# Attention and two expert layers on one core: sums of blocks taken one at a time, attention's late parts moved two points on, weight events spaced wider, another order in the opening

## The chip, the cores and the metric

The kernel runs on one core of a Trainium2 chip. The metric is the device time of one execution in microseconds (us). Engines run side by side, each through its own list of instructions in order: TensorE (PE; its weight loads are PEld), VectorE (DVE), ScalarE (ACT), GpSimd (POOL) and SyncE (SP), which here issues every DMA.

## The reference, cut to what matters

```python
# q, k, v: (4, 8, 768, 64); 8 memory slots ahead of each window; chunks of 32 queries
for c in range(24):                       # a chunk sees 8 + 16 + 32 + 8 = 64 slots
    scores = matmul(q_c, k_full.T) / 8
    out[:, :, chunk c] = softmax(scores) @ v_full
x = out.transpose(0, 2, 1, 3).reshape(3072, 512)
h = x @ w_in;  x = relu(h)**2 @ w_out     # first layer, w_in 512 x 2048, w_out 2048 x 512
h = x @ w_in2; g = h * tanh(softplus(h))  # second layer
return g @ w_out2
```

All in 32 bit. The weights are drawn as 64 bit numbers, and the kernel turns them into 32 bit ones itself.

## The kernel before, in words

**Blocks and steps.** The 3072 tokens are three blocks of 1024. Attention works in 12 pairs `p` of two 128-token tiles, four pairs to a block. After an opening (attention of pairs 0 to 3) come 48 steps `s`: 24 of the first layer, 24 of the second, eight per block, numbered `j`; each takes 256 of the 2048 columns. A matrix product is done as a 2x2 product of blocks with seven multiplications in place of eight, so there are sums of blocks before (T1 to T4 of the activations, S1 to S4 of the weights) and after. Each factor is split into a rounded part `hi` and a rest `lo`, and hi*hi, lo*hi and hi*lo are added up: six matmuls of 512 columns for a half product.

**One step.** `step(s)` writes the first product of step s between the second product of step s-1. PE's order is P1, P6, P5, P2, P7, P4, P3 (`product`, line 478, six matmuls each). P1 and P2 share PSUM bank 0 (`a`), P6, P7 and P4 bank 1 (`b`), P5 and P3 bank 2 (`c`). ACT copies `u1` from `a` (L737) before P2 may add to it; DVE makes `u2` (L744) and `u3` (L763) from `b`, each before the next product may add to `b`; then c22, c21, c12 (L765, L771, L776). `gate` applies the activation on ACT, casts `hi` (L491), and POOL subtracts to get `lo` (L492). In the first layer the second product is eight `unit`s (L533) with a DVE add into `y` (L547); in the second it is seven `product2` (L568) of blocks B11, B22, B21, T3, T1, T2, T4, each into one of two bank pairs. DVE adds a bank pair into a running block `m` (L556), or ACT copies it (L579) where j is 0. Three of the seven blocks are in buffers named by `spare` ('xt0' to 'xt2' or 'raw0' to 'raw2'), four in 'y0' and 'y1'. `sums_g` (L519) makes the T blocks of g on DVE.

**Combining.** When a block of tokens ends, seven additions over the `m` blocks give the four output blocks (`combine`, also L556, m<-m). Four stand behind the sixth product2 of the step after the block's last, three in the step after that, behind its first three product2. In the last step all seven come before `last_unit` (L607), which adds the last contribution unblocked, 12 matmuls for each output block, in bank pairs.

**Points.** A step has 15 points, the calls of `rest()` behind each product and unit. At a point, waiting stores and weight streams are issued, and then whatever `at(s, i)` listed: attention of later pairs (`plan_attention`) and weight events (`plan_w`), in the order in which they were listed (weights first). The order on each engine is that of the program text; no scheduler moves anything. First-layer points: P1 0, P6 1, P5 2, units 3 and 4, P2 5, P7 6, units 7 to 9, P4 10, P3 11, units 12 to 14; the gate of c21 comes behind point 10, that of c12 behind point 11.

**Attention of a pair.** `scores` (L344) on PE; maxima and exponentials; `normalize` (sums on DVE, multiplications on POOL, L384); `transpose_p` (L392) on PE; `copy_pt` (L402) on ACT; `values` (L414) on PE; `copy_x` (L426) on ACT; sums on POOL; a store. Scores, transposes and values share banks 6 and 7. In the opening `place_x` (L446 on ACT, L447 on DVE) puts a pair's blocks into x.

**A weight event** turns one matrix slice into hi and lo: `rebias` (A, a; ACT, L145) and `decode` (D, d; DVE, L152 to L156) of its halves, block sums (S, s; DVE, L167 to L171), casts (R, r; ACT, L211), subtractions (L, l; DVE, L218) and two pairs of stores. For the second layer's weights there are 16 events: six in steps 8 to 13, one each (both casts in one buffer, 'xt2'), and ten from step 17 on, one every nine points.

Of the kernel before, what the change touches and what calls it, by code (L numbers as in the profile page):

```python
# [41 lines left out]
PRODUCTS2 = [(A11, B11), (S4, B22), (A12, B21), (S3, T3), (S1, T1), (S2, T2), (A22, T4)]  # L42
STEPS = 2 * NSB * NQ

OUTPUTS = {T4: (1, 0), B21: (0, 0), T1: (1, 1), B22: (0, 1)}
FIRST2 = NSB * NQ
# [5 lines left out]
def tile_chunk_attention_moe_moe2(  # L52
# [224 lines left out]
    def spare(sb, i):  # L277

        return f"{('xt', 'raw')[sb % NSB % 2]}{i % 3}"
# [96 lines left out]
    def normalize(p):  # L376
        for h2 in range(2):
            nc.vector.tensor_reduce(out=r_t[p][:, h2], in_=p_t[p][:, h2], axis=AX.X, op=ALU.add)
        r = r_t[p]
        nc.vector.tensor_scalar_add(out=r, in0=r, scalar1=1.0e-9)  # L380
        nc.vector.reciprocal(out=r, in_=r)  # L381
        for h2 in range(2):
            pr = p_t[p][:, h2]
            nc.gpsimd.tensor_tensor(  # L384
                out=pr, in0=pr, in1=r[:, h2].unsqueeze(2).to_broadcast([128, 8, SLOTS]), op=ALU.mult
            )
# [197 lines left out]
    def combine(sb, blk, store):  # L584

        m = {b: m_t[sb, b] for _, b in PRODUCTS2}
        if blk == T2:
            add(m[T2], m[T2], m[B11])
            add(m[T3], m[T3], m[T2])
            add(m[T2], m[T2], m[T1])  # L590
            add(m[T1], m[T1], m[T3])
        else:
            add(m[blk], m[blk], m[{T4: T3, B22: T2, B21: B11}[blk]])
        if store:
            store_y(sb, *OUTPUTS[T1 if blk == T2 else blk], m[T1 if blk == T2 else blk])

    def last_unit(s, n):
# [4 lines left out]
        first = (4 + 2 * (pairs[0] % 2), 4 + 2 * ((pairs[0] + 1) % 2), 0, 2)[n]  # L602
# [35 lines left out]
    def at(s, i, *work):  # L638

        beside.setdefault((s + i // POINTS, i % POINTS), []).extend(work)  # L640

    def plan_attention(s, i, p):

        for n, work in {
# [5 lines left out]
            11: lambda: transpose_p(p),  # L650
            12: lambda: copy_pt(p),
            14: lambda: (values(p), load_q(p + 1) if (p + 1) % PSB else None),
            15: lambda: copy_x(p),
            16: lambda: sums_x(p, nc.gpsimd),
            20: lambda: store_x(p),
# [20 lines left out]
    def step(s):  # L676
# [44 lines left out]
        def done(i):  # L721
            _, sb, j = where(s - 1)
            final = s == STEPS - 1
            if (j == NQ - 1 or final) and PRODUCTS2[i][1] == T2:
                combine(sb, T2, not final)
            if final and PRODUCTS2[i][1] == T4:
                for blk in (T4, B22, B21):
                    combine(sb, blk, False)
            if sb > NSB and j == 0 and i < 3:
                combine(sb - 1, (T4, B22, B21)[i], True)  # L730

        if live:
# [59 lines left out]
    with tc.manual_schedule():  # L792
# [24 lines left out]
        def multiply(p):  # L817
            values(p)
            copy_x(p)
            sums_x(p, nc.vector if p == PSB - 1 else nc.gpsimd)  # L820
# [26 lines left out]
        normalize(3)  # L847
        turn(2)
        multiply(2)
        place_x(1, 0, 3)  # L850
        place_x(1, 3, 7)
        turn(3)
        multiply(3)
        place_x(2, 0, 3)
        place_x(2, 3, 7)
        place_x(3, 0, 3)
# [13 lines left out]
        for n, e in enumerate(seconds):  # L870
            if n < NQ - 2:
                plan_w(NQ + n, 0, e, "Aa|D|d|RS|s|L||||r|l", lambda e, i: round_w2(e, i, "xt2"), split_w2, "val")
            else:
                n -= NQ - 2
                hi = (["xt0", "xt1"], ["xt2", "at1"])[n % 2]
                plan_w(
                    2 * NQ + 1, 9 * n, e, "Aa|D|d|RS|s|Lr||l",
# [92 lines left out]
```

## Time and profile before

| what | value |
|---|---|
| median of three runs | 1168.34 us (1166.24 to 1169.35) |
| profiled execution | 1169.24 us, of it 1167.2 us from its first to its last instruction |
| mean granted clock of TensorE | 0.972 |
| PE busy | 1079.9 us (93%) |
| PEld busy | 881.1 us (75%) |
| DVE busy | 896.1 us (77%) |
| ACT busy | 561.5 us (48%) |
| POOL busy | 430.0 us (37%) |
| DMA | 324.94 MB, mean 278 GB/s |

Busy shares are averages over stages that differ. A timeline row gives the start, the time to the end of the last instruction of the group, engine, line, operation, names, shapes and count; in brackets stands the idle time before it and what ended it. A clock of 1.00 is 2.4 GHz; the other level is 1.2 GHz.

### The profile page before, as it was taken

What the parts mean: (1) busy time and instruction counts of PE and PEld (TensorE: products, weight loads), DVE (VectorE), ACT (ScalarE), POOL (GpSimd) and SP (SyncE); (2) the same over time, 40 slices, a digit from 0 to 9 for tenths busy, and PEclk for the clock granted to TensorE, in tenths of its full rate; (3) what the DMA queues carried; (4) which work ended last, traced back from release to release, by engine and by line L of the source; (5) the groups of instructions that cost most, each with busy time, mean ns of one, the idle gap of its engine ahead of it and who ended that gap; (6) DMA issues with size and microseconds to landing.
All of it is one profiled execution on the core that took longest, in us unless ns stands there. A gap on an engine that the chain in (4) does not pass through costs nothing.

```text
span 1167.2 us, 19779 instructions
## 1 busy us (share of the span) xinstructions
PE 1079.9 (93%) x7478; PEld 881.1 (75%) x7478; DVE 896.1 (77%) x1164; ACT 561.5 (48%) x879; POOL 430.0 (37%) x333
## 2 busy tenths in 40 slices
PE   6869899898799889999999999999989999799997
PEld 5748688776677778887777778888868888578885
DVE  5586879969666655678998677898878988768886
ACT  2467555555454444557565645444354443253331
POOL 2423223232223323223222244555355545245451
PEclk9999899999989889999999999999999999899998
DMA  9556867777998786869999958989997889867531
GB/s 359 231 193 233 293 214 262 260 277 248 384 320 315 263 292 241 280 237 395 342 338 329 362 218 289 314 304 339 345 309 276 303 304 391 277 207 230 161 128 72
DMA packets 192125, 324.94 MB, mean 278 GB/s; under 512 B 13344, under 2 KB 151072, under 8 KB 188192
## 3 DMA queue, kind: packets, MB, share of 16 engines
q1 hardware_dynamic: 192032, 323.69, 78.0%
q8 instruction: 60, 0.98, 0.3%
q14 instruction: 33, 0.27, 0.1%
HBM read 231.62 MB, written 92.01 MB: 277 GB/s over the span
## 4 chain that ended last, share of the span: by engine, by line
PE 56%; DVE 11%; DMA 7%; ACT 4%; issue 3%; SPq 0%; DVEq 0%; ACTq 0%
PE banks L478 26%; PE banks L568 17%; PE banks L533 10%; DMA w_d<-hi 2%; DVE m L556 2%; DVE y L547 1%; PE banks L414 1%; PE banks L607 1%; DMA w1s<-w_d 1%; DVE ty L632 1%; DVE val L152 1%; DVE r L519 1%; ACT r L497 1%; DMA xt<-xt_d 1%; DMA w2s<-w_d 1%
## 5 line engine op out<-in xcount | busy, mean ns | idle before, releaser
L478 PE MATMUL banks<-x,w1s 128*128 128x512 f32 x2016 | 507.8, 399 | 23.5 <-DVE u L763 7.5
L492 POOL TENSOR_TENSOR g<-r,g 128x512 fp32r<-128x512 f32 x206 | 287.3, 1401 | 537.5 <-ACT g L491 442.6
L478 PEld LDWEIGHTS banks<-x,w1s 128*128 128x128 f32 x2016 | 385.8, 193 | 112.5 <-DVE u L763 9.7
L533 PE MATMUL banks<-g,w2s 128*128 128x512 f32 x1152 | 282.4, 395 | 6.8 <-DVE y L547 5.3
L533 PEld LDWEIGHTS banks<-g,w2s 128*128 128x128 f32 x1152 | 217.2, 190 | 57.7 <-DVE y L547 8.2
L568 PE MATMUL banks<-g,w2s 128*128 128x512 f32 x966 | 241.3, 392 | 9.8 <-ACT m L579 7.6
L568 PEld LDWEIGHTS banks<-g,w2s 128*128 128x128 f32 x966 | 181.2, 189 | 52.2 <-ACT m L579 9.7
L556 DVE TENSOR_TENSOR m<-banks,m 128x1024 f32<-128x1024 f32 x144 | 173.6, 1218 | 34.9 <-PE banks L568 26.3
L491 ACT CAST g<-r 128x512 fp32r<-128x512 f32 x206 | 127.0, 621 | 37.5 <-DVE r L519 30.3
L547 DVE TENSOR_TENSOR y<-banks,y 128x512 f32<-128x512 f32 x168 | 112.0, 682 | 39.0 <-PE banks L533 38.9
L492 POOL TENSOR_TENSOR g<-more,g 128x512 fp32r<-128x512 f32 x55 | 79.7, 1453 | 81.0 <-ACT g L491 66.6
L497 ACT ACTIVATE r<-r 128x512 f32<-128x512 f32 x72 | 45.4, 631 | 69.7 <-DVE r L771 50.1
L501 ACT ACTIVATE r<-r 128x512 f32<-128x512 f32 x48 | 30.4, 632 | 71.4 <-DVE r L771 35.9
L211 ACT CAST hi<-val 128x1024 fp32r<-128x1024 f32 (+1 forms) x32 | 30.4, 949 | 69.5 <-DVE val L156 50.5
L498 ACT ACTIVATE r<-r 128x512 f32<-128x512 f32 x96 | 60.7, 632 | 3.1
L152 DVE TENSOR_SCALAR val<-val 128x512 f32<-128x512 f32 x64 | 38.9, 607 | 26.5 <-ACT val L145 26.4
L414 PE MATMUL banks<-pt,v 64*64 64x32 f32 x1536 | 39.9, 262 | 19.4 <-ACT pt L402 19.0
L218 DVE TENSOR_TENSOR val<-val,hi 128x1024 f32<-128x1024 f32 (+1 forms) x32 | 37.2, 1162 | 25.2 <-ACT hi L211 25.0
L414 PEld LDWEIGHTS banks<-pt,v 64*64 64x64 f32 x1536 | 37.0, 185 | 25.7 <-ACT pt L402 24.8
L737 ACT COPY u<-banks 128x512 f32<-128x512 f32 x48 | 28.1, 585 | 52.0 <-PE banks L478 52.0
L384 POOL TENSOR_TENSOR p<-p,sum 128x512 f32<-128x512 f32 x24 | 28.7, 1215 | 63.3 <-DVE sum L381 25.0
L344 PE MATMUL banks<-k,q 64*32 64x64 f32 x1536 | 37.5, 250 | 13.2 <-DMA k<-k_dram 7.1
(71 smaller groups left out, 999.9 us busy)
## 6 DMA issues: line engine op xcount, KB each, us to landing
w1s<-w_d SPq DMA_DIRECT2D x280, 256.0 KB, 5.4
w2s<-w_d SPq DMA_DIRECT2D x229, 256.0 KB, 5.3
raw<-w_dram SPq DMA_DIRECT2D x64, 512.0 KB, 5.0
w_d<-w1s SPq DMA_DIRECT2D x8, 1792.0 KB, 7.5
x<-xs_d SPq DMA_DIRECT2D x14, 1024.0 KB, 10.7
k<-k_dram SPq DMA_DIRECT2D x24, 512.0 KB, 7.0
v<-v_dram SPq DMA_DIRECT2D x24, 512.0 KB, 8.9
xt<-xt_d SPq DMA_DIRECT2D x21, 512.0 KB, 7.3
```

The lines of the kernel that those rows point to most:

```text
L152: nc.vector.tensor_scalar(out=val, in0=val, scalar1=LIMIT, scalar2=-LIMIT * NEGATIVE, op0=ALU.min, op1=ALU.max)
L344: nc.tensor.matmul(out=s4[32 * c:32 * c + 32, j, hp, :], lhsT=q_t[p][r0:r0 + 64, j, hp, 32 * c:32 * c + 32], rhs=k_t[p][r0:r0 + 64, j, hp, ...
L414: nc.tensor.matmul(out=x_ps[par][64 * h2:64 * h2 + 64, o:o + 32], lhsT=v_t[p][j][r0:r0 + 64, h2, a, c, :], rhs=pt_t[p][r0:r0 + 64, h2, j, ...
L478: nc.tensor.matmul(out=ps, lhsT=w[:, a, f:f + 128], rhs=x[:, xi, c, kk, :], start=start and i == 0, stop=stop and i == len(order) - 1, ski ...
L491: nc.scalar.copy(out=g[:, 0], in_=r)
L492: nc.gpsimd.tensor_tensor(out=g[:, 1], in0=r, in1=g[:, 0].bitcast(FP32), op=ALU.subtract)
L497: nc.scalar.activation(out=r, in_=h, func=ACTF.Relu)
L498: nc.scalar.activation(out=r, in_=r, func=ACTF.Square)
L533: nc.tensor.matmul(out=ps, lhsT=w[:, a, blk(f), d % 2 * 128:d % 2 * 128 + 128], rhs=g_t[s, (f, t)][:, c, :], start=i == 0, stop=i == len(o ...
L547: nc.vector.tensor_tensor(out=y, in0=ps, in1=y, op=ALU.add)
L556: engine.tensor_tensor(out=to, in0=in0, in1=in1, op=ALU.add)
L568: nc.tensor.matmul(out=bank(first + d), lhsT=w[:, a, 128 * d:128 * d + 128], rhs=g[:, c, :], start=i == 0, stop=i == 2)
```

## The change

- `PRODUCTS2`: the products of T1 and T2 change places (T2 fifth, T1 sixth).
- `combine` does one addition per call, listed in `SUMS`. At a block's end the first stands behind product T2, the second behind T1; in the next step the third stands behind `sums_g` of T2 and the other four behind product2 of B11, B22, B21 and T3. In the last step: one behind T2, three behind T1, three behind T4.
- `spare` counts blocks from the second layer's first, so the last block's three `m` go to 'raw' and no longer to 'xt'.
- `last_unit` takes banks 0 to 3 first and the two bank pairs last.
- Attention in steps: transposes, copy_pt one point later, values, copy_x, sums and store two later, load_q one earlier. The first point and period go from 4 and 26 to 4 and 25 (from step 0), and from 10 and 19 to 8 and 19 (from step 9). There q is now loaded ahead of k.
- Weight events: seven in steps 8 to 14, nine from step 17 on, one every ten points.
- Opening: pair 3's normalizing and pair 2's sums go from POOL to DVE; the placing of pairs 1 and 2 goes behind values(3), ahead of copy_x(3); pair 3's first part is placed ahead of its sums.

```diff
-PRODUCTS2 = [(A11, B11), (S4, B22), (A12, B21), (S3, T3), (S1, T1), (S2, T2), (A22, T4)]
+PRODUCTS2 = [(A11, B11), (S4, B22), (A12, B21), (S3, T3), (S2, T2), (S1, T1), (A22, T4)]
+SUMS = [(T2, B11), (T3, T2), (T2, T1), (T1, T3), (T4, T3), (B22, T2), (B21, B11)]
...
-        return f"{('xt', 'raw')[sb % NSB % 2]}{i % 3}"
+        return f"{('xt', 'raw')[(sb - NSB) % 2]}{i % 3}"
...
-    def combine(sb, blk, store):
+    def combine(sb, to, other, store=False):
 
         m = {b: m_t[sb, b] for _, b in PRODUCTS2}
-        if blk == T2:
-            add(m[T2], m[T2], m[B11])
-            add(m[T3], m[T3], m[T2])
-            add(m[T2], m[T2], m[T1])
-            add(m[T1], m[T1], m[T3])
-        else:
-            add(m[blk], m[blk], m[{T4: T3, B22: T2, B21: B11}[blk]])
-        if store:
-            store_y(sb, *OUTPUTS[T1 if blk == T2 else blk], m[T1 if blk == T2 else blk])
+        add(m[to], m[to], m[other])
+        if store and (to, other) in SUMS[3:]:
+            store_y(sb, *OUTPUTS[to], m[to])
...
-        first = (4 + 2 * (pairs[0] % 2), 4 + 2 * ((pairs[0] + 1) % 2), 0, 2)[n]
+        first = (0, 2, 4 + 2 * (pairs[0] % 2), 4 + 2 * ((pairs[0] + 1) % 2))[n]
...
-            11: lambda: transpose_p(p),
-            12: lambda: copy_pt(p),
-            14: lambda: (values(p), load_q(p + 1) if (p + 1) % PSB else None),
-            15: lambda: copy_x(p),
-            16: lambda: sums_x(p, nc.gpsimd),
-            20: lambda: store_x(p),
+            12: lambda: transpose_p(p),
+            13: lambda: (copy_pt(p), load_q(p + 1) if (p + 1) % PSB else None),
+            16: lambda: values(p),
+            17: lambda: copy_x(p),
+            18: lambda: sums_x(p, nc.gpsimd),
+            22: lambda: store_x(p),
...
-            if (j == NQ - 1 or final) and PRODUCTS2[i][1] == T2:
-                combine(sb, T2, not final)
-            if final and PRODUCTS2[i][1] == T4:
-                for blk in (T4, B22, B21):
-                    combine(sb, blk, False)
-            if sb > NSB and j == 0 and i < 3:
-                combine(sb - 1, (T4, B22, B21)[i], True)
+            blk = PRODUCTS2[i][1]
+            if s == STEPS - 1:
+                for n in {T2: (0,), T1: (1, 2, 3), T4: (4, 6, 5)}.get(blk, ()):
+                    combine(sb, *SUMS[n])
+            elif j == NQ - 1:
+                for n in {T2: (0,), T1: (1,)}.get(blk, ()):
+                    combine(sb, *SUMS[n])
+            elif sb > NSB and j == 0:
+                for n in {B11: (3,), B22: (4,), B21: (5,), T3: (6,)}.get(blk, ()):
+                    combine(sb - 1, *SUMS[n], store=True)
...
+                if where(s - 1)[1] > NSB and where(s - 1)[2] == 0:
+                    combine(where(s - 1)[1] - 1, *SUMS[2])
...
-        def multiply(p):
+        def multiply(p, *others):
             values(p)
+            for other in others:
+                place_x(*other)
             copy_x(p)
-            sums_x(p, nc.vector if p == PSB - 1 else nc.gpsimd)
+            if p == PSB - 1:
+                place_x(p, 0, 3)
+            sums_x(p, nc.vector if p >= PSB - 2 else nc.gpsimd)
...
-        normalize(3)
+        normalize(3, nc.vector)
         turn(2)
         multiply(2)
-        place_x(1, 0, 3)
-        place_x(1, 3, 7)
         turn(3)
-        multiply(3)
-        place_x(2, 0, 3)
-        place_x(2, 3, 7)
-        place_x(3, 0, 3)
+        multiply(3, (1, 0, 3), (1, 3, 7), (2, 0, 3), (2, 3, 7))
         place_x(3, 3, 7)
...
-            if n < NQ - 2:
+            if n < NQ - 1:
...
-                    2 * NQ + 1, 9 * n, e, "Aa|D|d|RS|s|Lr||l",
+                    2 * NQ + 1, 10 * n, e, "Aa|D|d|RS|s|Lr||l",
...
-            start, first, period = ((0, 4, 26), (NQ + 1, 10, 19))[sb]
-            at(start, 0, *([lambda p=p: load_k(p)] if sb else []), lambda p=p: load_q(p))
+            start, first, period = ((0, 4, 25), (NQ + 1, 8, 19))[sb]
+            at(start, 0, lambda p=p: load_q(p))
+            if sb:
+                at(start, 0, lambda p=p: load_k(p))
```

## Rows read from the trace of the kernel before

**Rows 1.** Windows of stages: stretch, length, busy us (count) per engine, clock, DMA share, GB/s
```profile
62.20:468.40 406.20, 369.37 (x3495) 299.17 (x3496) 297.05 (x461) 215.06 (x343) 124.48 (x108) 0.95 0.76 271
468.40:509.20 40.80, 40.80 (x182) 33.78 (x181) 26.16 (x33) 23.18 (x35) 10.31 (x9) 1.00 0.72 249
509.20:662.30 153.10, 146.74 (x631) 118.57 (x630) 133.13 (x208) 88.17 (x136) 37.05 (x27) 0.99 0.95 346
```

**Rows 2.** Windows of steps 11, 33, 41 and 43, same columns
```profile
359.10:389.20 30.10, 26.58 (x231) 22.19 (x227) 17.93 (x31) 14.21 (x23) 8.76 (x8) 0.89 0.83 296
840.10:865.80 25.70, 21.69 (x85) 16.62 (x84) 21.41 (x20) 12.70 (x18) 11.73 (x7) 0.93 0.74 244
1000.20:1030.00 29.80, 21.98 (x86) 17.02 (x85) 18.11 (x19) 12.85 (x18) 9.35 (x7) 0.89 0.71 235
1049.00:1068.00 19.00, 19.00 (x85) 15.74 (x84) 15.85 (x17) 7.25 (x12) 9.85 (x7) 1.00 0.61 194
```

**Rows 3.** Timeline of PE, second layer
```profile
858.62 4.50 PE L478 MATMUL banks<-x,w1s 128*128 128x512 f32 x12 [3.17 <-DVE u L763]
...
1015.89 2.93 PE L568 MATMUL banks<-g,w2s 128*128 128x512 f32 x6 [6.36 <-ACT m L579]
...
1151.24 11.04 PE L607 MATMUL banks<-g,w2s 128*128 128x512 f32 x36 [3.84 <-DVE m L556]
```

**Rows 4.** Timeline of DVE, the combining sums of steps 32, 33 and 41
```profile
840.22 5.01 DVE L556 TENSOR_TENSOR m<-m 128x1024 f32<-128x1024 f32 x4
...
851.22 6.74 DVE L556 TENSOR_TENSOR m<-m 128x1024 f32<-128x1024 f32 x3
...
1011.25 3.48 DVE L556 TENSOR_TENSOR m<-m 128x1024 f32<-128x1024 f32 x3
```

**Rows 5.** Timeline of POOL, steps 32 and 33
```profile
825.14 3.45 POOL L492 TENSOR_TENSOR g<-r,g 128x512 fp32r<-128x512 f32 x2
...
852.44 2.24 POOL L492 TENSOR_TENSOR g<-more,g 128x512 fp32r<-128x512 f32 x1
```

**Rows 6.** Timeline of ACT, step 41
```profile
1014.83 1.01 ACT L579 COPY m<-banks 128x1024 f32<-128x1024 f32 x1 [6.41 <-DVE m L556]
```

**Rows 7.** Timeline of DVE, the end
```profile
1144.32 5.72 DVE L556 TENSOR_TENSOR m<-m 128x1024 f32<-128x1024 f32 x4
...
1162.32 1.23 DVE L556 TENSOR_TENSOR m<-banks,m 128x1024 f32<-128x1024 f32 x1 [1.49 <-PE banks L607]
```

**Rows 8.** Timelines of ACT, DVE and PE, the end of the opening
```profile
59.66 3.47 ACT L446 CAST x<-stage 128x768 fp32r<-128x768 f32 x4
...
61.28 4.09 DVE L447 TENSOR_TENSOR x<-stage,x 128x768 fp32r<-128x768 f32 x4
...
62.24 7.20 PE L478 MATMUL banks<-x,w1s 128*128 128x512 f32 x18 [3.57 <-ACT x L446]
```

**Rows 9.** Timeline of PE, waits of the first layer
```profile
84.90 1.07 PE L392 MATMUL banks<-cst,p 128*128 128x128 f32 x4 [4.41 <-POOL p L384]
...
140.63 4.12 PE L414 MATMUL banks<-pt,v 64*64 64x32 f32 x128 [3.25 <-ACT pt L402]
...
382.81 1.46 PE L414 MATMUL banks<-pt,v 64*64 64x32 f32 x30 [3.45 <-ACT pt L402]
...
...
420.05 4.12 PE L414 MATMUL banks<-pt,v 64*64 64x32 f32 x128 [3.21 <-ACT pt L402]
...
560.15 3.01 PE L478 MATMUL banks<-x,w1s 128*128 128x512 f32 x12 [2.21 <-ACT u L737]
```

**Rows 10.** Timeline of ACT, steps 11 and 13
```profile
377.39 1.05 ACT L211 CAST hi<-val 128x1024 fp32r<-128x1024 f32 x1 [3.20 <-DMA w_d<-hi]
...
418.31 1.22 ACT L145 ACTIVATE val<-raw 128x512 f32<-128x512 f32 x2 [5.85 <-DMA w_d<-val]
...
424.27 1.07 ACT L426 COPY stage<-banks 128x512 f32<-128x512 f32 x2 [0.19 <-DMA raw<-w_dram]
```

**Rows 11.** Timeline of ACT, step 19
```profile
558.78 0.83 ACT L211 CAST hi<-val 128x768 fp32r<-128x768 f32 x1 [3.94 <-DVE val L156]
```

More of the change, by code (lines that the diff above doesn't have):

```diff
@@ L374, in exps, with normalize @@
         nc.scalar.activation(out=pr, in_=pr, func=ACTF.Exp, scale=scale)
-    def normalize(p):
+    def normalize(p, engine=nc.gpsimd):
         for h2 in range(2):
@@ L383, in normalize @@
             pr = p_t[p][:, h2]
-            nc.gpsimd.tensor_tensor(
+            engine.tensor_tensor(
                 out=pr, in0=pr, in1=r[:, h2].unsqueeze(2).to_broadcast([128, 8, SLOTS]), op=ALU.mult
@@ L722, in done @@
             _, sb, j = where(s - 1)
-            final = s == STEPS - 1
-            if (j == NQ - 1 or final) and PRODUCTS2[i][1] == T2:
-                combine(sb, T2, not final)
-            if final and PRODUCTS2[i][1] == T4:
-                for blk in (T4, B22, B21):
-                    combine(sb, blk, False)
-            if sb > NSB and j == 0 and i < 3:
-                combine(sb - 1, (T4, B22, B21)[i], True)
+            blk = PRODUCTS2[i][1]
[8 more added lines that the diff above has]
+                    combine(sb - 1, *SUMS[n], store=True)
         if live:
@@ L870, in tile_chunk_attention_moe_moe2 @@
         for n, e in enumerate(seconds):
-            if n < NQ - 2:
+            if n < NQ - 1:
                 plan_w(NQ + n, 0, e, "Aa|D|d|RS|s|L||||r|l", lambda e, i: round_w2(e, i, "xt2"), split_w2, "val")
             else:
-                n -= NQ - 2
+                n -= NQ - 1
                 hi = (["xt0", "xt1"], ["xt2", "at1"])[n % 2]
                 plan_w(
-                    2 * NQ + 1, 9 * n, e, "Aa|D|d|RS|s|Lr||l",
+                    2 * NQ + 1, 10 * n, e, "Aa|D|d|RS|s|Lr||l",
                     lambda e, i, hi=hi: round_w2(e, i, hi[i]), split_w2, ("val", "at0")[n % 2],
```

## The prediction

> **What bounds the kernel now.** I read the page's shares first: PE is busy 93% of the span, so a gain has to come from PE's waits, from the lower clock that follows some of them, or from the two ends. Then the windows by stage, to see which stages lie above their floor. The reader is to see in [rows 1] that two steps without attention or weight events take 40.8 us, 20.40 each, with PE never idle; that is the floor of a first-layer step (90 matmuls, 0.227 us each). Seven steps with weight events take 153.1, where 7 x 20.40 = 142.8: 10.3 us too long. The first stretch, steps 0 to 14, has a granted clock of 0.95 over 406.2 us: about 41 us of it at 1.2 GHz. In the second layer a step takes 19.0 us [rows 2], but step 33 takes 25.7 and step 41 takes 29.8. Third, PE's timeline gives the waits behind these numbers [rows 3, 9]; fourth, the timelines of DVE, POOL and ACT say what ended them [rows 4 to 8, 10, 11].
>
> The sums are made against the profiled execution, 1169.24 us (span 1167.2 and 2.0 around it). It lies 0.9 above the median of 1168.34, so 0.9 comes off at the end.
>
> **The end (step 47 and the last unit).** Now four sums (5.72 us), one addition of a bank pair (1.23, the length of the last one) and three sums stand in DVE's list one after the other from 1144.32; PE waits 3.84 us for a bank pair and then takes 11.04 us for 36 matmuls [rows 3, 7], which at 0.227 us would take 8.2: it runs at the lower clock. DVE's last addition ends at 1163.55. After: the first two output blocks go to banks that nobody reads any more, so PE has no wait, and the other 24 matmuls need only the pair that the T1 addition frees. DVE then sets the end: one of the four early sums is done before, so from the T1 addition's end it has 6 sums and 5 additions of 1.23 = 13.5 us, plus 0.7 because the first sums run beside POOL (5.72 against 4 x 1.23 = 4.9). That addition ends at 1144.3, so DVE ends near 1158.5 to 1159.2: 4.3 to 5 us earlier. The stores now come 1.23 apart, which may cost some of it. I take **-4.3** (bounds -5.5 and -2).
>
> **Steps 33 and 41.** In step 32 four sums (5.01 us) stand ahead of the T4 addition and of the sums_g that start step 33; three more, 6.74 us, end just before u3, and PE waits 3.17 us for u3 [rows 3, 4]. In step 41 the wait is another: the copy of m waits for the old m in the same 'xt' buffer (6.41 us on ACT, 6.36 on PE) [rows 3, 6]; its three sums take only 3.48. The new `spare` removes that sharing, so step 41 becomes a second step 33. There, the first sum goes before the T1 addition, where DVE has time (15.85 us busy in a 19.0 us step [rows 2]); the second stays ahead of the T4 addition; the third to sixth stand ahead of u3, the seventh behind c22. So the chain up to u3 loses two sums ahead of the T4 addition and the one behind c22, and gets two back in step 33: it starts some 3.7 us earlier (three sums of 1.25) and has one more sum in it.
>
> What that one costs depends on POOL. A sum takes 1.16 us where POOL stood still and 2.25 where POOL was subtracting [rows 4]; in that stretch a subtraction itself took 2.24 us [rows 5]. With all four sums at 2.25, u3 comes 3.7 - 2.25 = 1.4 us earlier, so step 33 gains 1.4 and step 41, from 29.8 to 24.3, gains 5.5: -6.9. With all at 1.16 the wait vanishes and both steps fall to 19.0: -17.4. POOL has five subtractions in this stretch, so I take the near end: **-7** (bounds -17.4 and -3). The Trainium skill's page "SBUF — State Buffer", section "Who interferes with whom", says that a DVE instruction with both inputs in SBUF contends with a GpSimd instruction that reads SBUF, and that the loser is held for the whole of the other. The trace agrees in kind (2.25 and 2.24 against 1.16 us), and by the rule the far end cannot be reached.
>
> The exchange of T1 and T2 I cost at nothing: T2's product comes one product (1.36 us) earlier, 9 products or 12.2 us into the step, and POOL has finished its subtraction 7.5 us after the step's start (PE began step 32 at 821.1, and the two subtractions that end with it run from 825.14 for 3.45 us [rows 5]). Were that cover gone, each 0.1 us would cost 2.3 us over 23 steps.
>
> **Weight events from step 17 on.** The typical wait is step 19's: an event nine points behind another starts at point 12, so its first cast stands at point 0 in ACT's list ahead of u1; it waits 3.94 us for DVE's decode [rows 11], and P2, which needs u1, waits 2.21 [rows 9]. Steps 19 and 22 are of this kind. With a spacing of ten, events start at points 0, 10 and 5 alone; only the last cast of the second kind falls on point 0, and its data are due one point earlier than step 19's were. I estimate u1 at 5 us into the step, where P2 needs it after 30 matmuls, 6.8 us. One event fewer also takes a tenth off a DMA load that is busy 0.95 of the time [rows 1]. Of the 10.3 us I take **-6** (bounds -10.3 and 0).
>
> **Attention in steps 1 to 6.** Pair 4's transposes move behind P6: the 4.41 us wait [rows 9] is covered by six more matmuls, 1.4 us (2.4 at the lower clock). Pair 5's values move from the end of step 2 behind step 3's P1: 1.4 of 3.25 us. DVE's backlog behind both stays. With something of the clock, **-4.5** (bounds -11 and +3).
>
> **Attention in steps 9 to 14.** In step 11 ACT's cast waited for a store until 377.39, then the gate of c21 came, and only then copy_pt, for which PE waited 3.45 us [rows 9, 10]. copy_pt at point 10 stands ahead of that gate: ready at 377.39 + 1.05 + 1.07 = 379.5 in place of 382.8, 3.3 us, and of a clock of 0.89 over 30.1 us (3.3 us lost [rows 2]) most comes back: -6. In step 13 copy_pt stood behind a rebias that waited 5.85 us for a store, and PE waited 3.21 [rows 9, 10]; it moves to the end of step 12, ahead of the rebias. But the next pair's scores now come two points behind copy_x and no longer four, in the same banks. copy_x ends at 425.34 [rows 10], 12.8 us into the step (which began 18 matmuls before that wait, at 412.5), held by the same rebias; PE would be there after 36 matmuls and the values (2.06 at full clock, half of 4.12 [rows 9]), at 10.2: a new wait of 2.6. Net -1.5. Step 14 gets an event that it hadn't: pair 11's copy_pt at point 3 stands behind its first cast, by step 13's measure 12.7 us in, and PE wants it at 10.5: +2.2. In step 9 the scores come two points earlier and k is issued behind q: between -4 and +6, taken as -0.7. Sum **-6** (bounds -16 and +8).
>
> **The opening.** P1 waits for ACT's third cast behind copy_x(3); after, only one cast stands there, 2/4 of 3.47 = 1.7 us earlier or somewhat more. But P6 and DVE's decode need the last placing, and DVE's placing takes 4.09 us for four parts [rows 8], of which two are now done before: 2 us earlier. Multiplying on DVE lies where DVE was idle, waiting for copy_x. **-1.5** (bounds -3.2 and 0).
>
> **Sum.** -4.3 - 7 - 6 - 4.5 - 6 - 1.5 = -29.3: 1139.9 by the profile, 1139 by the median.
>
> **The rivals.**
> - *Attention's waits only change their place.* Values wait less, but scores wait for copy_x and step 14 for its event; the two attention terms come to nothing, 10.5 us less: 1150. For it: ACT's casts that wait for stores stay where they are. Against it: in step 11 the order on ACT alone removes the wait.
> - *POOL holds every sum, and the last units too.* If each of the four sums ahead of u3 waits for a whole subtraction, step 33 gains nothing in place of 1.4, step 41 gains 4 in place of 5.5 and the end 3 in place of 4.3: 1143. For it: 2.25 us against 1.16 [rows 4]. Against it: POOL has gaps between its five subtractions. It is what the rule of the Trainium skill named above makes of this kernel, and the trace bears it out where POOL was busy.
> - *More than that.* PE stays at 2.4 GHz through steps 1 to 14 (41 us at 1.2 GHz cost 20 now; half of them beyond the terms above is 10) and the sums fall into POOL's gaps (17.4 in place of 7): 1119. Against it: both need a chain on DVE that the change hardly shortens.
> - *Slower.* ACT's list in steps 9 to 14: copy_x of a pair stands behind a cast that waits for the store of the cast before it (3.20 us of wait now [rows 10]), and two points on PE needs the banks for the next scores. If copy_x comes 8 us behind PE's need in steps 11, 13 and 14, and k does so in step 9, each wait costs 8 us and half as much again by the lower clock: four are 48. Against them stand the waits of steps 11 and 13 that go (3.45 + 3.21, and half again: 10) and the terms of the second layer, its events and the end (17.3): 1168.3 + 48 - 27.3 = 1189. It decides from 27.3 / 6 = 4.5 us a wait. Against it: the store's wait is 3 to 6 us now, and part of it lies ahead of PE's need.
> - *The change doesn't do what it says*: DVE's order in step 33 is as late as before. That is inside the second rival, since step 41's buffer and the end don't hang on it.
>
> **How the numbers follow.** Forecast 0.46 (1139, its own range 1130 to 1147), attention's waits moved 0.22 (1150), every sum held 0.12 (1143), more than that 0.13 (1119), slower 0.07 (1189, with times from 1165 on). About 0.3%, 3.5 us, is what a measurement can tell from no change. Slower by more gets 0.06, within 0.3% 0.05, faster 0.89. The range 1120 to 1157 takes in the first three cases and half of the fourth, with the bounds of the two terms of attention.
>
> **What would show it.** The copy of m in step 41 no longer waiting for DVE, and steps 33 and 41 of equal length near 24 us; sums at 2.2 us beside POOL; the last 36 matmuls without a wait; copy_pt in step 11 ahead of a gate; steps 18 to 22 within 1 us of 20.4 each. Wrong would be: waits of scores for copy_x over 4 us, a wait of P2 for u1 in step 14, product2 of T2 waiting for POOL in ordinary steps, or steps 33 and 41 at 19 us.

## The result, and the profile after

The changed kernel takes 1126.64 us (median of 4 runs, 1125.83 to 1131.35), the kernel before 1167.29 beside it (4 runs, 1166.01 to 1169.35): a ratio of 0.966, 95% interval 0.963 to 0.969. The forecast was 1139, in a range of 1120 to 1157. The sum was made from one profiled execution to another, 1169.24 to 1126.08: it said -29.3 us, and -43.2 came. The medians differ by 40.7; the profiled execution of the kernel before was one of its longer ones.

The windows of the changed kernel, by stage: stretch, length, busy us (count) of PE, PEld, DVE, ACT and POOL, granted clock, DMA share, GB/s. The stretches are steps 0 to 14, 15 and 16, 17 to 23, steps 11, 33, 41 and 43, steps 1 to 6, steps 9 to 14.

```profile
61.40:452.90 391.50, 362.12 (x3494) 294.46 (x3495) 300.20 (x475) 217.42 (x347) 127.62 (x107) 0.97 0.80 286
452.90:494.10 41.20, 41.14 (x181) 33.71 (x180) 25.92 (x33) 23.62 (x36) 10.83 (x9) 1.00 0.78 277
494.10:637.40 143.30, 143.12 (x632) 118.22 (x631) 127.82 (x197) 87.54 (x136) 37.66 (x27) 1.00 0.99 355
354.20:377.70 23.50, 23.50 (x227) 19.59 (x226) 17.61 (x30) 12.47 (x20) 8.02 (x6) 1.00 0.97 346
812.80:835.00 22.20, 19.67 (x85) 15.61 (x84) 19.56 (x18) 12.20 (x18) 11.58 (x8) 1.00 0.64 215
969.40:991.50 22.10, 19.60 (x86) 15.59 (x85) 19.40 (x18) 12.15 (x18) 11.45 (x8) 1.00 0.63 214
1010.50:1029.50 19.00, 19.00 (x85) 15.75 (x84) 15.84 (x17) 7.25 (x12) 9.84 (x7) 1.00 0.60 193
78.80:239.30 160.50, 150.39 (x1501) 123.66 (x1500) 137.13 (x215) 96.10 (x155) 59.66 (x49) 0.96 0.70 257
288.80:452.90 164.10, 152.74 (x1645) 125.72 (x1644) 111.67 (x182) 85.31 (x140) 55.12 (x49) 0.96 0.91 324
```

The last two stretches before, same columns:

```profile
79.00:245.20 166.20, 152.72 (x1501) 124.31 (x1500) 139.54 (x215) 96.32 (x155) 56.22 (x49) 0.95 0.69 249
295.40:468.40 173.00, 157.24 (x1646) 129.64 (x1645) 107.02 (x171) 82.90 (x136) 55.42 (x50) 0.93 0.84 299
```

Set these against [rows 1, 2]. Steps 0 to 14 are 14.7 us shorter, 391.5 for 406.2. PE's idle time in them (length less busy) fell by 7.4, from 36.8 to 29.4, and its busy time by 7.3, from 369.4 to 362.1, for the same matmuls at a granted clock of 0.97 in place of 0.95: taken together, the waits that went gave about as much again through the clock. Steps 17 to 23 stand at their floor, 143.3 where 7 x 20.40 = 142.8. Step 33 went from 25.7 to 22.2, step 41 from 29.8 to 22.1, at a clock of 1.00. Steps 43 and 15 and 16, which the change doesn't touch, are as before within 0.4.

The terms, from the step lengths (first matmul of P1 to first matmul of P1) of the two traces:

| term | predicted | measured |
|---|---|---|
| opening and step 0 | -1.5 | -0.2 |
| steps 1 to 6 | -4.5 | -5.7 |
| steps 9 to 14 | -6 | -8.9 |
| weight events, steps 17 to 23 | -6 | -9.9 |
| step 24 | not in the sum | -2.3 |
| steps 33 and 41 | -7 | -3.5 and -7.7 |
| the end | -4.3 | -4.5 |
| all other steps | 0 | -0.4 |

PE's timeline of the changed kernel, rows that answer to [rows 3, 8, 9]: start, time, engine, line, operation, names, shapes, count, and in brackets the idle time before and what ended it.

```profile
61.43 2.93 PE L480 MATMUL banks<-x,w1s 128*128 128x512 f32 x6 [2.02 <-ACT x L448]
64.96 5.29 PE L480 MATMUL banks<-x,w1s 128*128 128x512 f32 x12 [0.60 <-ACT x L448]
...
84.37 2.93 PE L480 MATMUL banks<-x,w1s 128*128 128x512 f32 x6 [4.09 <-DVE r L771]
87.10 1.91 PE L394 MATMUL banks<-cst,p 128*128 128x128 f32 x8
...
137.28 0.30 PE L416 MATMUL banks<-pt,v 64*64 64x32 f32 x2 [1.89 <-ACT pt L404]
...
307.35 0.65 PE L346 MATMUL banks<-k,q 64*32 64x64 f32 x32 [2.56 <-DMA k<-k_dram]
313.83 0.31 PE L346 MATMUL banks<-k,q 64*32 64x64 f32 x1 [1.72 <-issue]
...
374.26 2.07 PE L416 MATMUL banks<-pt,v 64*64 64x32 f32 x128
...
412.62 0.81 PE L346 MATMUL banks<-k,q 64*32 64x64 f32 x43 [0.99 <-ACT stage L428]
...
439.44 0.30 PE L416 MATMUL banks<-pt,v 64*64 64x32 f32 x2 [1.07 <-ACT pt L404]
...
829.12 3.01 PE L480 MATMUL banks<-x,w1s 128*128 128x512 f32 x12 [2.53 <-DVE u L763]
...
985.61 3.01 PE L480 MATMUL banks<-x,w1s 128*128 128x512 f32 x12 [2.50 <-DVE u L763]
...
1105.72 11.04 PE L603 MATMUL banks<-g,w2s 128*128 128x512 f32 x48
```

The last row is the end: 48 matmuls without a wait at 0.23 us each, in the 11.04 us that 36 took before behind their wait of 3.84 [rows 3]. In step 11 the values (374.26) wait no more, and take 2.07 us.

ACT's timeline at the end of the opening and in steps 11 and 19, against [rows 8, 10, 11]:

```profile
63.87 1.04 ACT L448 CAST x<-stage 128x1024 fp32r<-128x1024 f32 x1 [2.49 <-DVE stage L438]
...
369.73 1.05 ACT L213 CAST hi<-val 128x1024 fp32r<-128x1024 f32 x1 [0.79 <-DMA w_d<-hi]
370.69 1.06 ACT L404 COPY pt<-banks 128x512 f32<-128x512 f32 x2
372.68 0.63 ACT L499 ACTIVATE r<-r 128x512 f32<-128x512 f32 x1 [0.93 <-DVE r L771]
...
538.86 0.56 ACT L735 COPY u<-banks 128x512 f32<-128x512 f32 x1
```

The first row is the last placing of the opening (below). copy_pt (370.69) stands ahead of the gate of c21 (372.68), as the forecast wanted it, and u1 of step 19 comes 3.5 us into the step (it began at 535.37), ahead of P2's need at 6.8.

DVE's timeline in step 33 and at the end, against [rows 4, 7]:

```profile
818.85 2.31 DVE L558 TENSOR_TENSOR m<-m 128x1024 f32<-128x1024 f32 x1
...
822.80 5.67 DVE L558 TENSOR_TENSOR m<-m 128x1024 f32<-128x1024 f32 x3
828.39 0.68 DVE L763 TENSOR_TENSOR u<-banks,u 128x512 f32<-128x512 f32 x1
...
1105.70 5.21 DVE L558 TENSOR_TENSOR m<-m 128x1024 f32<-128x1024 f32 x3
...
1112.08 3.50 DVE L558 TENSOR_TENSOR m<-m 128x1024 f32<-128x1024 f32 x3
1115.49 4.61 DVE L558 TENSOR_TENSOR m<-banks,m 128x1024 f32<-128x1024 f32 x4
```

Four sums stand ahead of u3 in step 33 (the one at 818.85 and the three from 822.80), 7.98 us of DVE, and PE's 2.53 us of wait follow from them. At the end DVE goes without a gap from 1105.70 to 1120.10, 14.4 us, where the forecast had 13.5 and 0.7.

### The profile page after: what moved, and what is told of

The parts are those of the page before. It is cut to its first block, busy times and chain, and to the rows that moved or that the text cites. A ratio compares the mean times of both kernels' runs of the same rounds, so it can differ in the third digit from the quotient of the medians.

```text
span 1124.2 us, 19766 instructions
## 1 busy us (share of the span) xinstructions
PE 1061.5 (94%) x7478; PEld 872.3 (78%) x7478; DVE 898.6 (80%) x1170; ACT 561.6 (50%) x879; POOL 430.5 (38%) x327
## 4 chain that ended last, share of the span: by engine, by line
PE 65%; DVE 14%; DMA 6%; issue 4%; ACT 3%; POOL 1%; SPq 0%; DVEq 0%; ACTq 0%; POOLq 0%
PE banks L480 29%; PE banks L535 16%; PE banks L570 15%; DVE m L558 3%; PE banks L416 1%; PE banks L346 1%; DVE r L521 1%; DMA w_d<-hi 1%; DMA w2s<-w_d 1%; DVE y L549 1%; DMA w1s<-w_d 1%; DVE ty L628 1%; DVE val L157 1%; DVE val L158 1%; DVE val L154 1%
## 5 line engine op out<-in xcount | busy, mean ns | idle before, releaser
L480 PE MATMUL banks<-x,w1s 128*128 128x512 f32 x2016 | 502.2, 396 | 19.1 <-DVE u L763 7.3
L558 DVE TENSOR_TENSOR m<-banks,m 128x1024 f32<-128x1024 f32 x144 | 173.3, 1218 | 30.5 <-PE banks L570 27.5
L549 DVE TENSOR_TENSOR y<-banks,y 128x512 f32<-128x512 f32 x168 | 111.4, 682 | 25.7 <-PE banks L535 25.4
L346 PEld LDWEIGHTS banks<-k,q 64*32 64x32 f32 x1536 | 33.4, 125 | 21.5 <-issue 18.2
L158 DVE SCALAR_TENSOR_TENSOR val<-raw,val 128x512 uint32<-128x512 uint32 x64 | 47.3, 738 | 2.2
L386 POOL TENSOR_TENSOR p<-p,sum 128x512 f32<-128x512 f32 x22 | 25.6, 1186 | 57.8 <-DVE sum L383 23.3
L416 PE MATMUL banks<-pt,v 64*64 64x32 f32 x1536 | 35.1, 249 | 11.3 <-ACT pt L404 9.8
```

Of the source, the lines that this page charges most:

```text
L158: nc.vector.scalar_tensor_tensor(out=vb, in0=low, scalar=29, in1=vb, op0=ALU.logical_shift_right, op1=ALU.bitwise_or)
L346: nc.tensor.matmul(out=s4[32 * c:32 * c + 32, j, hp, :], lhsT=q_t[p][r0:r0 + 64, j, hp, 32 * c:32 * c + 32], rhs=k_t[p][r0:r0 + 64, j, hp, ...
L416: nc.tensor.matmul(out=x_ps[par][64 * h2:64 * h2 + 64, o:o + 32], lhsT=v_t[p][j][r0:r0 + 64, h2, a, c, :], rhs=pt_t[p][r0:r0 + 64, h2, j, ...
L480: nc.tensor.matmul(out=ps, lhsT=w[:, a, f:f + 128], rhs=x[:, xi, c, kk, :], start=start and i == 0, stop=stop and i == len(order) - 1, ski ...
L549: nc.vector.tensor_tensor(out=y, in0=ps, in1=y, op=ALU.add)
L558: engine.tensor_tensor(out=to, in0=in0, in1=in1, op=ALU.add)
```

## Experiments

Theory A is the forecast's account part by part; theory B, where it differs, is told in each expectation. Ratios are to the kernel before, run on the same chip. Steps 1 to 6 and 9 to 14 need care: the profiled executions of nine kernels with the new points of attention there took 155.6 to 160.7 in steps 1 to 6 (mean 158.7), five with the old points 162.3 to 166.3 (164.4); in steps 9 to 14 it is 163.2 to 166.9 (165.8) and 164.5 to 173.0 (170.4). So steps 9 to 14 gain 4.5 us by these means, half of the 8.9 of the one pair above. The other stretches agree much better, steps 33 and 41 apart (below).

**The kernel before with one part each.** First, the buffers of the running blocks alone:

```diff
-        return f"{('xt', 'raw')[sb % NSB % 2]}{i % 3}"
+        return f"{('xt', 'raw')[(sb - NSB) % 2]}{i % 3}"
```

> The kernel before with the new buffer names alone (last block's m in 'raw'). Theory A, the shared 'xt' buffer is what makes step 41 longer than step 33: step 41 falls from 29.8 us to step 33's 25.7, step 33 stays, the time falls by 4 us. Theory B, the seven sums in DVE's list hold step 41 whatever the buffer: it stays within 1 us of 29.8.

Ratio 0.9965 (0.9945 to 0.9984), 10 runs. Its windows of steps 33 and 41:

```profile
831.00:856.70 25.70, 21.68 (x85) 16.59 (x84) 21.30 (x20) 12.68 (x18) 11.73 (x7) 0.93 0.75 247
991.10:1016.80 25.70, 21.68 (x85) 16.59 (x84) 21.31 (x20) 12.68 (x18) 11.72 (x7) 0.93 0.74 244
```

The two steps are now equal, 25.7, so step 41's excess of 4.1 [rows 2] was the shared buffer. A.

Second, the spacing of the weight events alone:

```diff
-            if n < NQ - 2:
+            if n < NQ - 1:
...
-                n -= NQ - 2
+                n -= NQ - 1
...
-                    2 * NQ + 1, 9 * n, e, "Aa|D|d|RS|s|Lr||l",
+                    2 * NQ + 1, 10 * n, e, "Aa|D|d|RS|s|Lr||l",
```

> The kernel before with seven weight events in steps 8 to 14 and nine at a spacing of ten points from step 17 on. Theory A, the place of the casts in ACT's list and the lighter load from step 17 on: steps 17 to 23 fall from 153.1 us to 143 (each 20.4), step 24 from 22.7 to 20.4 because the last event's stores no longer lie in front of its loads, step 14 grows by 1 to 2 us: 10 to 12 us faster in all. Theory B, the gain there needs the earlier attention too: under 5 us.

Ratio 0.9932 (0.9906 to 0.9958). Windows of steps 17 to 23 and of step 24:

```profile
505.30:648.20 142.90, 142.90 (x631) 118.14 (x630) 127.95 (x197) 87.73 (x136) 37.89 (x28) 1.00 0.99 356
648.20:668.60 20.40, 20.40 (x91) 16.89 (x90) 13.92 (x18) 10.42 (x15) 6.26 (x5) 1.00 0.75 253
```

PE is never idle in either. The whole excess of 10.2 us goes, and step 24 falls from 22.7 to 20.4 with it. Step 14, which has the event more, took 23.55, no longer than before (23.84). A, by these steps; the median fell by 8.6 us, a little under the 10 to 12 that A had said. Place and number of the events changed together here, so what each of them gives isn't shown.

Third, the points of attention alone:

```diff
-            11: lambda: transpose_p(p),
...
+            12: lambda: transpose_p(p),
...
-            start, first, period = ((0, 4, 26), (NQ + 1, 10, 19))[sb]
+            start, first, period = ((0, 4, 25), (NQ + 1, 8, 19))[sb]
```

> The kernel before with attention's new points and periods alone. Theory A, the order on ACT and PE frees steps 2, 11 and 13: steps 1 to 6 together 5 us shorter, step 11 down by 6.5 us to 23.5, step 13 down by 5.5 to 26.5, step 14 unchanged at 23.8 (no event in it); in all 15 to 17 us faster. Theory B, the waits move to other places unless the opening starts earlier: under 8 us.

Ratio 0.987 (0.9836 to 0.9903), the largest of the parts. Steps 1 to 6 took 156.8 and 9 to 14 163.2; step 11 24.5, step 13 25.85. A.

Fourth, the opening alone:

```diff
-        normalize(3)
+        normalize(3, nc.vector)
...
-        multiply(3)
...
+        multiply(3, (1, 0, 3), (1, 3, 7), (2, 0, 3), (2, 3, 7))
```

> The kernel before with the new opening alone. Theory A, DVE's backlog eats the earlier start: step 0 begins 0.8 us earlier, and nothing of it is left after step 0; time within 1.5 us of before. Theory B, it sets DVE's backlog in steps 1 to 3 and with it the 12 us that step 2 lost: 4 us faster or more.

Ratio 0.9975 (0.9949 to 1.0001): not told from no change, as A had it. P1 starts at 61.4 in place of 62.2, and step 0 is 0.6 longer.

**The changed kernel with one thing back.** The sums in groups again, with the new buffers and banks (four behind T1, three in the next step):

```diff
-                for n in {T2: (0,), T1: (1,)}.get(blk, ()):
-                    combine(sb, *SUMS[n])
+                for n in {T1: (0, 1, 2, 3)}.get(blk, ()):
+                    combine(sb, *SUMS[n], store=True)
...
-                for n in {B11: (3,), B22: (4,), B21: (5,), T3: (6,)}.get(blk, ()):
+                for n in {B11: (4,), B22: (5,), B21: (6,)}.get(blk, ()):
...
-                if where(s - 1)[1] > NSB and where(s - 1)[2] == 0:
-                    combine(where(s - 1)[1] - 1, *SUMS[2])
```

> The changed kernel with the sums of a block's end grouped again (four behind the sixth product, three behind the first three of the next step); the last step, the buffers and all else as changed. Theory A, splitting them is worth what is left of steps 33 and 41 after the buffer's part: both grow from 22.1 us to 25.7, the time by 7 us. Theory B, the splitting is worth nothing and steps 33 and 41 are shorter for the buffer alone: both stay near 22.

Ratio 0.9731 (0.9702 to 0.976). Windows of steps 33 and 41:

```profile
813.00:838.60 25.60, 21.71 (x86) 16.62 (x84) 21.23 (x20) 12.68 (x18) 11.73 (x7) 0.93 0.77 252
972.90:998.50 25.60, 21.73 (x86) 16.62 (x85) 21.50 (x20) 12.72 (x18) 11.72 (x7) 0.93 0.73 237
```

Taking the sums one at a time is worth 3.4 us in each of the two steps (25.6 to 22.2); the rest of step 41's gain is the buffer. A.

The banks of the last units as before:

```diff
-        first = (0, 2, 4 + 2 * (pairs[0] % 2), 4 + 2 * ((pairs[0] + 1) % 2))[n]
+        first = (4 + 2 * (pairs[0] % 2), 4 + 2 * ((pairs[0] + 1) % 2), 0, 2)[n]
```

> The changed kernel with last_unit's banks as before (the pairs first). Theory A, DVE sets the end and the banks only spare PE a wait that is hidden behind DVE: time within 1 us of the changed kernel. Theory B, the banks are the gain at the end: PE waits 3 us or more again for a pair, falls to the lower clock, and the end is 4 us later.

Ratio 0.9718 (0.9675 to 0.9762). PE in step 33, and at the end:

```profile
830.51 4.61 PE L480 MATMUL banks<-x,w1s 128*128 128x512 f32 x12 [2.48 <-DVE u L763]
...
1116.08 11.07 PE L603 MATMUL banks<-g,w2s 128*128 128x512 f32 x36 [3.24 <-DVE m L558]
```

B: the gain at the end is the banks. The wait is back (3.24, before 3.84) with the slow 36 matmuls behind it, and step 47 takes 41.4, 3.9 more than the 37.5 of the changed kernel. The first row matters for the next part: the wait of 2.48 is that of the changed kernel, but the 12 matmuls behind it take 4.61 us and not 3.01, so they ran in part at 1.2 GHz, and the step takes 23.4.

Two of the sums moved behind later products (both were meant to be ones that stand ahead of u3):

```diff
-                for n in {B11: (3,), B22: (4,), B21: (5,), T3: (6,)}.get(blk, ()):
+                for n in {B11: (3,), B22: (4,), T3: (5,), T1: (6,)}.get(blk, ()):
```

> The changed kernel with two of the four sums that stand ahead of u3 in steps 33 and 41 moved behind it (B22's behind product T3, B21's behind product T1). Theory A, the wait for u3 (2.5 us in each) is the length of DVE's list ahead of u3: it goes, steps 33 and 41 fall from 22.1 us to 19.1 to 20.2, 4 to 6 us in all; the copy of T3's m may wait about 1 us. Theory B, u3 waits for POOL's or ACT's chain: the steps stay within 0.5 us of 22.1.

Ratio 0.9674 (0.9647 to 0.9701). PE in step 33:

```profile
830.29 1.88 PE L480 MATMUL banks<-x,w1s 128*128 128x512 f32 x7 [1.39 <-DVE u L763]
```

Steps 33 and 41 take 21.03 and 20.99, 1.1 less each. I had expected 19.1 to 20.2 by A, and the miss is a reading of my own edit: only one sum left the stretch ahead of u3, the one of 1.2 us beside which POOL stood still. The other had been behind u3 already. The wait fell by 1.14, that one sum.

**What holds the sums.** POOL's five subtractions in steps 33 and 41 replaced by zeros that POOL writes, so that it writes as much and reads nothing; the lo parts of g are left out of these two steps:

```diff
+        if apart[0]:
+            nc.gpsimd.memset(g[:, 1].bitcast(FP32), 0.0)
+            return
         nc.gpsimd.tensor_tensor(out=g[:, 1], in0=r, in1=g[:, 0].bitcast(FP32), op=ALU.subtract)
...
+            apart[0] = s in (FIRST2 + NQ + 1, FIRST2 + 2 * NQ + 1)
```

> The changed kernel, in which POOL's subtractions in steps 33 and 41 are replaced by writing zeros (so the lo parts of g are left out there). Theory A, DVE's sums are held by POOL's reads: without them each sum takes 1.2 us in place of 2.2, u3 comes some 4 us earlier, the wait of 2.5 us goes and both steps fall from 22.1 to 19.1 us. Theory B, POOL's instructions as such (writes too) hold them, or the sums are slow for another reason: they stay near 2.2 us and the steps near 22.

One run, 1122.55. DVE, POOL and the window of step 33:

```profile
820.23 1.22 DVE L562 TENSOR_TENSOR m<-m 128x1024 f32<-128x1024 f32 x1
...
822.57 3.49 DVE L562 TENSOR_TENSOR m<-m 128x1024 f32<-128x1024 f32 x3
```

```profile
815.91 1.46 POOL L496 MEMSET g<- 128x512 f32 x3
819.70 1.00 POOL L496 MEMSET g<- 128x512 f32 x2 [2.33 <-PE banks L574]
...
825.14 0.53 POOL L496 MEMSET g<- 128x512 f32 x1 [2.19 <-PE banks L574]
```

```profile
815.30:834.40 19.10, 19.10 (x86) 15.79 (x85) 15.57 (x19) 12.87 (x18) 4.12 (x8) 1.00 0.79 264
```

Each of the four sums takes 1.22 us (three in a row 3.49), PE has no wait, and the step is at its floor. POOL's writes are shorter than its subtractions (0.53 against 1.3 us and more), so the step's time alone doesn't part reading from being busy for less time; but the write at 825.14 lies wholly within the last of the three sums (824.84 to 826.05), which took 1.22 us as the others did. A: POOL's subtractions cost DVE's four sums 3.3 us (7.98 less 4.71). The Trainium skill's page "SBUF — State Buffer", section "Who interferes with whom", says that DVE with two SBUF inputs contends with a GpSimd instruction that reads SBUF and not with one that only writes it; these rows agree.

**A version that could be better.** One sum alone between u2 and u3:

```diff
-                for n in {T2: (0,), T1: (1,)}.get(blk, ()):
+                for n in {T2: (0,), T1: (1, 2)}.get(blk, ()):
...
-                for n in {B11: (3,), B22: (4,), B21: (5,), T3: (6,)}.get(blk, ()):
+                for n in {B11: (3,), T3: (4, 5), T1: (6,)}.get(blk, ()):
...
-                if where(s - 1)[1] > NSB and where(s - 1)[2] == 0:
-                    combine(where(s - 1)[1] - 1, *SUMS[2])
```

> The changed kernel with the sum T2+T1 taken in the block's last step, behind product T1, where POOL stands still, and with T4's and B22's sums behind product T3 and B21's behind T1, so that one sum alone stands between u2 and u3 in steps 33 and 41. Theory A, the wait for u3 is DVE's list with POOL's reads in it: u3 ends 12.2 us into the step, ahead of PE's need at 13.6; no wait for u3, and what is left is a wait of 0.3 to 1.7 us of the sixth product2 for the copy of T3's m, which waits for B22's sum: steps of 19.4 to 20.7 us, 3 to 5.5 us faster than the changed kernel. Theory B, moved sums only hold c21 and the copies instead: steps stay at 21 us or more.

Median 1124.22 (5 runs, 1122.97 to 1125.6), ratio 0.9654 (0.9624 to 0.9683). The window of step 33, then PE and ACT in it:

```profile
813.30:834.40 21.10, 19.40 (x86) 15.70 (x85) 19.46 (x18) 11.70 (x17) 11.46 (x8) 1.00 0.69 234
```

```profile
831.49 1.67 PE L570 MATMUL banks<-g,w2s 128*128 128x512 f32 x6 [1.70 <-ACT m L581]
```

```profile
830.43 1.93 ACT L581 COPY m<-banks 128x1024 f32<-128x1024 f32 x2 [3.12 <-DVE m L558]
```

u3 is no longer waited for. In its place ACT's copy into `m` waits 3.12 us for a sum that reads the old block, and PE waits 1.70 for that copy to free the bank pair. The step gains 1.1, as much as with the version before: A was right on u3, B on the step (21.07, where A had 19.4 to 20.7). It is the fastest median of all the versions that leave nothing out, but its interval overlaps that of the changed kernel: only the two step lengths tell them apart.

**Attention's halves.** The old points and first point for pairs 8 to 11 (steps 9 to 14), with k ahead of q there (`soon` lists the old points, `late` the new ones):

```diff
-            12: lambda: transpose_p(p),
...
+            **(late if p < 2 * PSB else soon)(p),
...
-            start, first, period = ((0, 4, 25), (NQ + 1, 8, 19))[sb]
+            start, first, period = ((0, 4, 25), (NQ + 1, 10, 19))[sb]
```

> The changed kernel with the old points, start and load order for pairs 8 to 11 (steps 9 to 14) alone. Theory A, the new points matter there: step 11 grows from 23.5 to 24.4 us back to 26 to 30, step 13 from 26 to 28.7 back to 29 to 33; steps 9 to 14 together 4 to 9 us longer. Theory B, most of the shorter time of steps 9 to 14 is the spread between executions: within 2 us.

Ratio 0.9734 (0.969 to 0.9778). PE in step 11, and the window of steps 9 to 14:

```profile
371.58 0.30 PE L416 MATMUL banks<-pt,v 64*64 64x32 f32 x2 [3.48 <-ACT pt L404]
```

```profile
285.50:457.90 172.40, 157.79 (x1645) 130.31 (x1645) 115.19 (x182) 85.84 (x140) 55.26 (x50) 0.93 0.88 312
```

The wait of 3.45 [rows 9] is back as 3.48, the clock as 0.93, and step 11 takes 30.5, step 13 32.4. A.

The old points and period for pairs 4 to 7 (steps 1 to 6):

```diff
+            **(late if p >= 2 * PSB else soon)(p),
...
-            start, first, period = ((0, 4, 25), (NQ + 1, 8, 19))[sb]
+            start, first, period = ((0, 4, 26), (NQ + 1, 8, 19))[sb]
```

> The changed kernel with the old points and period for pairs 4 to 7 (steps 0 to 6) alone. Theory A, the move of pair 5's values out of step 2 is what shortens steps 1 to 6: step 2 grows from 21.6 back to some 33 us and step 3 falls to 25, steps 1 to 6 together 5 to 8 us longer. Theory B, the opening's earlier start did it: within 2 us.

Ratio 0.9722 (0.9685 to 0.9759). PE at pair 5's values, and the window of steps 1 to 6:

```profile
139.46 0.30 PE L416 MATMUL banks<-pt,v 64*64 64x32 f32 x2 [3.25 <-ACT pt L404]
```

```profile
78.20:241.90 163.70, 149.70 (x1502) 121.75 (x1502) 140.13 (x215) 96.45 (x155) 56.23 (x49) 0.97 0.70 252
```

The wait of 3.25 [rows 9] is back, and the stretch is 3 us longer than in the changed kernel, 5 longer than the mean of the nine executions with the new points (158.7). Steps 2 and 3 took 32.9 and 24.3, as A had it; of its 5 to 8 us for the stretch it is the small end at most.

Last, k loaded ahead of q in step 9 again:

```diff
-            at(start, 0, lambda p=p: load_q(p))
             if sb:
                 at(start, 0, lambda p=p: load_k(p))
+            at(start, 0, lambda p=p: load_q(p))
```

> The changed kernel with k loaded ahead of q at the start of step 9, as before. Theory A, k's landing is what holds pair 8's scores (waits of 2.6 and 0.5 us in step 9): k is issued some 0.5 us earlier, the waits fall by 0.5 to 1.5 us. Theory B, the scores wait as long for q or for the instructions of PE then: step 9 stays at 35 to 36 us.

Ratio 0.9686 (0.9643 to 0.973). PE in step 9:

```profile
307.41 0.81 PE L346 MATMUL banks<-k,q 64*32 64x64 f32 x43 [2.78 <-DMA q<-q_dram]
```

Step 9 takes 36.01 us, as in the changed kernel (that the digits agree is chance): now the scores wait 2.78 us for q, where they waited 2.56 and 0.54 for k. B: which of the two comes first makes no difference, since the scores need both.

## Why the prediction was right, and where not

The time lies within the stated range, but under the forecast's own 1130 to 1147: most steps of the account held, and several terms were too small.

**Right, by its own steps.** The end came as worked out (-4.3 and -4.5): the banks take PE's wait away, and DVE's list of 14.4 us sets the end. Step 41 is a second step 33 once the buffer is no longer shared. In step 11 the order on ACT removes the wait, and the half clock goes with it (-6 and -6.6; by the means of the nine and five executions -4.6). ACT's cast came 2.8 us earlier in the step as well; had it not, the values would have waited some 0.4 us, an estimate from the lengths of these rows. The events leave steps 17 to 23 at their floor. The exchange of T1 and T2 cost nothing: the ordinary second-layer steps are unchanged at 19.04.

**Steps 33 and 41: the step that failed is the clock.** The forecast had four sums ahead of u3 at 2.25 us, and both steps near 24. DVE's part was close: three sums took about 2.3 and one 1.2, and u3 began 15.6 us into step 33 in place of 17.8, 2.2 earlier where 1.4 was said. (The wait fell by less, from 3.17 to 2.53, because PE now comes there sooner.) But the forecast took for granted that PE runs at 1.2 GHz behind that wait, as behind 3.17 [rows 3]. In the changed kernel it doesn't: 12 matmuls in 3.01 us, clock 1.00. That is the other 1.3 of step 33's 3.5 us, and it was luck: of the ten steps 33 and 41 in five kernels with this wait (2.48 to 2.53 us), five took 22.1 to 22.2 us and five 23.3 to 23.5, among them both of the kernel with the old banks, where 12 matmuls took 4.61 us. What decides is open. The far end of the bounds (both steps at 19.0) is what happens when POOL doesn't read, as the zeros showed; the rival that POOL holds every sum fell too, since one of the four ran free, and both steps gained more than its 0 and 4 us.

**The weight events: a term of the right mechanism, too small.** Spared were 9.9 of some 10.2 us, not 6. The sum left room for u1 at 5 us into the step; it came at 3.5, and no P2 waits. The second reason given, a tenth off the DMA load, came out otherwise: the bytes of steps 17 to 23 fell by 4% (52.9 to 50.8 MB), and the DMA share rose from 0.95 to 0.99. Step 24's -2.3 wasn't in the sum at all. Before, PE waited there for u1 and u2; first ACT in step 23, then PE in step 24:

```profile
652.39 1.05 ACT L273 CAST x<-xt 128x1024 fp32r<-128x1024 f32 x1 [6.70 <-DMA xt<-xt_d]
...
670.15 1.67 PE L478 MATMUL banks<-x,w1s 128*128 128x512 f32 x6 [0.88 <-ACT u L737]
```

The last event's last store was issued 3.1 us into step 23, and the loads of the next block's x behind it; ACT's first cast of that x came 10.5 us into the step, and such casts still stood ahead of u1 in step 24. In the changed kernel the store goes out at 0.3 and the cast comes at 7.7, and PE waits for neither u1 nor u2.

**Steps 1 to 6: the total near, one of its two parts wrong.** The 1.4 us for pair 4's transposes behind P6 failed (nor do six matmuls take 2.4 us at the lower clock: P6 took 2.93). The wait of 4.41 for POOL's multiplication [rows 9] is gone, but P6, which now stands first, waits 4.09 for DVE to read bank `b` (c21 of step 0). That wait had lain behind the other one. Step 1 is 1.5 longer than before. The gain is pair 5's: its values behind step 3's P1 wait 1.89 in place of 3.25, and steps 2 and 3 together fall from 59.5 to 52.7. Over the whole stretch PE's idle time fell by 3.4 and its busy time by 2.3.

**Steps 9 to 14: a cost that didn't come.** In step 13 the forecast set a new wait of 2.6 us for copy_x against what was gained, and took -1.5; the wait is 0.99 and the step gains 5.5. Of the 5.5, 2.2 are the waits (3.21 less 0.99) and the rest the clock behind them, for which the forecast's -1.5 leaves 0.9. The forecast's wait was too long by 1.6 because copy_x ended 12.0 us into the step and not 12.8, because PE went on after the first of its two copies (0.5), and because PE itself came there 0.4 later than worked out. Step 14 came as forecast in kind (+2.2 said, +1.4 measured, a wait of 1.07 for pt), but it takes both causes together: with the event and the old points, or the new points without the event, the step took 23.55. Step 9 lost 1.1 where -0.7 was said. By the means of the nine and five executions steps 11 and 13 give 8.9 us (28.6 to 24.0 and 31.4 to 27.1), and steps 9, 10 and 14 take back 4.3.

**The opening: -1.5 failed.** P1 does start 0.8 earlier, behind a wait of 2.02. But P6, which needs the last placing, then waits 0.60 more and begins at 64.96; before, by P1's 2.93 us, it began near 65.2 (62.24 and 2.93), so hardly anything of the lead is left. Behind that second wait 12 matmuls take 5.29 us, at 1.2 GHz, and the scores behind them begin at 70.19, where they had begun at 69.37. The step that failed is the last placing 2 us earlier: ACT's cast of it ended at 64.91, where it had ended at 63.13 [rows 8]. It now waits 2.49 us (63.87) for pair 3's sums on DVE, and these stand behind the placing that was moved ahead of them. Some comes back at u3, whose wait fell from 1.88 to 0.88.

**The rivals.** That attention's waits only change their place held in step 1, and for about half of what steps 11 and 13 gave. "More than that" was nearer in time than it was given credit for, but not by its own mechanism: of the 13.9 us beyond the sum 6.2 are the events with step 24, which it didn't have, 4.2 steps 33 and 41, where one sum fell into POOL's gap and the clock was lucky, and 2.9 steps 9 to 14, which lie within the spread.

**What stays open** beside the clock: steps 1 to 6 and 9 to 14 vary by several us between executions of the same code, so each half's gain, some 5.7 and 4.5 us by the means, is known only to 2 or 3. The means are of kernels that differ in other parts of the change too.

## What to carry to other kernels

Where a stage has a floor that undisturbed steps show, and the part of the kernel that disturbs it is moved off the path, the whole excess can go, and some of the steps behind the stage with it; the events gave all 10 us where this forecast took 6, and 2 more one step on. Before a wait is called covered by the work put ahead of it, look what that work itself waits for: the wait behind the wait takes its place. A buffer or bank that is shared by name alone is worth looking for, since another buffer in one place and another order of banks in the other cost nothing here and gave about 4 us each.

## What the runs showed of the hardware

A sum of 128x1024 on DVE takes 1.22 us (three in a row 3.48 to 3.50), and up to 2.31 beside POOL's subtraction; beside POOL's writes alone it took 1.22. The granted clock behind a wait of 2.5 us differed between executions of the same code around it (1.00 in the changed kernel's step 33, 1.2 GHz for a stretch with the old banks). And the short matmuls of the scores stand still without any wait on another engine that the profile shows, 1.72 us in the changed kernel and 3.07 in the last experiment ("issue"), both in step 9. What PE waited for there isn't settled.
